# Fourteen tiles of x are turned by VectorE from square blocks instead of by TensorE, and the stage for v runs in the order in which it is written

## The chip, the cores and the metric

The kernel runs on one core of a Trainium2 chip. The metric is the device time of one execution in microseconds; three executions of the kernel before give a median of 1278.13 us (1277.75 to 1278.33).

The engines are called by the names of the profile: PE (matmuls on TensorE; PEld is its weight load), DVE (VectorE), ACT (ScalarE), POOL (GpSimd) and SP (SyncE, whose queue issues nearly all DMAs here). Each engine works through its own instructions in a fixed order.

## What is computed

One block of a network mixes two branches with a gate per token (B = 1, S = 2048 tokens, D = 512 channels, 32 heads of 16, F = 1792):

```python
x = A_x
g = _sigmoid((x * gate_w).sum(-1, keepdims=True))
a = _A_ref(x, A_wqkv, A_wo)                       # softmax attention, 32 heads of 16
b = _B_ref(x, B_w1, B_b1, B_w2, B_b2)             # layernorm, then an MLP across the tokens
return g * a + (1 - g) * b
```

What matters here is the beginning of it: `v = x @ wqkv[:, 1024:1536]`, and for each token the gate's sum `(x * gate_w).sum(-1)` and the mean and variance of its row. All matmul operands are float32 values split into a rounded part `hi` and a rest `lo`; a product is the sum of three matmuls, `hi*hi + hi*lo + lo*hi`.

## The kernel before

The 2048 tokens are 16 tiles of 128 rows. TensorE contracts over the partitions, so x is needed with its channels on the partitions: `xt_hi` and `xt_lo`, 128 partitions by 4 chunks of channels by 2048 tokens. They are kept, since the projections for k and q use them too.

The first stage makes them and v. For a tile t:

- `load(t)` brings the 128 rows of x, 2 KB each, as one DMA of 256 KB on SP's queue. Six buffers rotate; a buffer is free again when `row_stats` of its tile is done.
- `turn(t)` is four transposes of 128 by 128 on PE into one PSUM bank (line 201). `turned(t)` splits the bank: ACT copies it into `xt_hi` (line 82), DVE subtracts that from the bank into `xt_lo` (line 83).
- `products` adds up twelve matmuls of 512 columns (line 90) for v, three for each of the four chunks of channels. `v_out(t)` copies the bank into `v` on ACT (line 235).
- `row_stats(t)` on DVE reads the rows of x as they were loaded: BN_STATS (line 212), BN_AGGR (line 213) and a product with `gate_w` that also sums (line 215).

The weights for v come in four chunks of 128 channels, `wv_raw0` to `wv_raw3`, split by ACT and DVE into `wv_hi` and `wv_lo` (`split_wv`). Tiles 0 and 1 are done first and by hand: their matmuls (line 268, `part`) go chunk by chunk, in the order in which the weights arrive. This head is under `manual_schedule`, in which each engine's instructions stand in the order in which the program writes them. From tile 2 on the loop

```python
for t in range(2, NS):
    if t + 4 < NS: load(t + 4)
    if t + 1 < NS: turn(t + 1)
    if t == 4: biases(pool)
    if t in (8, 12): qk_w.append(wcols(qk_cols.pop(0)))
    row_stats(t - 2)
    ps = bank(); products(ps, v_pairs(t)); v_out(t, ps)
```

is left to a scheduler, which places each instruction when its operands can be there. It may pull a call forward out of its place in the text: POOL's fills of the two bias tiles (line 224), the two small loads of the biases (line 225) and the fill of `v` (line 296) are written late and stand early in their engines' order. In `biases` each of the two bias vectors is loaded into a cleared 128 by 128 tile, turned by a transpose on PE (line 227) and copied out by DVE (line 228).

`wcols` loads and splits the weights of one block of k or q, 128 columns as 512 pieces of 512 bytes (line 172). The stage after (line 90 again, `wc_hi` and `wc_lo`) projects k and q from `xt_hi` and `xt_lo`; then come the first layer of the MLP, attention with the rest of the MLP between its matmuls, and the output. None of that is touched.

Each DMA on SP's queue has one of eight semaphores in turn and waits for the DMA that had it before, so that at most eight are under way.

Of the kernel before, what the change touches and what calls it, by code (L numbers as in the profile page):

```python
# [10 lines left out]
F32 = mybir.dt.float32  # L11
# [4 lines left out]
ALU = mybir.AluOpType  # L16
# [6 lines left out]
P = 128  # L23
S = 2048
D = 512
F = 1792
H = 32
DH = 16
NS = S // P
ND = D // P  # L30
NF = F // P
NB = 512
NQ = S // NB
VC = DH + 1
SCALE = DH**-0.5
# [40 lines left out]
def gated_mix(ctx: ExitStack, tc: tile.TileContext, a_x, a_wqkv, a_wo, b_w1, b_b1, b_w2, b_b2, gate_w, out):  # L76
    nc = tc.nc
    xf, of = (t.rearrange("b s d -> (b s) d") for t in (a_x, out))

    def split(hi, lo, src, copy, sub):  # L80

        copy(hi, src)  # L82
        return sub(lo, src, hi.bitcast(F32), ALU.subtract)  # L83

    def products(ps, pairs, start=True, stop=True):

        n, last = 0, 3 * len(pairs) - 1
        for (lh, ll), (rh, rl) in pairs:
            for a, b in ((lh, rh), (lh, rl), (ll, rh)):
                nc.tensor.matmul(ps, a, b, start=start and n == 0, stop=stop and n == last)  # L90
                n += 1
# [7 lines left out]
    ident = const.tile([P, P], F32, name="ident")  # L99
# [3 lines left out]
    z = const.tile([P, NS], F32, name="z")  # L103
# [9 lines left out]
    v = v_pool.tile([P, NS, H, VC], F32, name="v")  # L113
# [21 lines left out]
    loaded, ready, subs = [], [], []  # L135
# [27 lines left out]

    qk = qk_ctx.enter_context(tc.tile_pool(name="qk", bufs=2, side="right"))

    def wcols(c0):
# [3 lines left out]
        src = a_wqkv[:, c0 : c0 + P].rearrange("(k p) c -> p k c", p=P)  # L170
        with tc.issue_after(x_load.ins):
            nc.sync.dma_start(raw, src)
        split(hi, lo, raw, nc.scalar.copy, nc.gpsimd.tensor_tensor)
        return hi, lo

    qk_cols = [c0 + b * P for b in range(ND) for c0 in (D, 0)]
    qk_w = []
    x_load = None

    with tc.tile_pool(name="vp", bufs=1, side="right") as pool:  # L180
        xs = {}

        def load(t):
            nonlocal x_load
            xs[t] = pool.tile([P, D], F32, name="x", bufs=6)
            x_load = nc.sync.dma_start(xs[t], xf[t * P : (t + 1) * P, :])  # L186

        gw = pool.tile([P, D], F32, name="gw")
        wv = []

        def load_wv(k):
            raw = pool.tile([P, D], F32, name=f"wv_raw{k}")
            nc.sync.dma_start(raw, a_wqkv[k * P : (k + 1) * P, 2 * D : 3 * D])  # L193
            wv.append((raw, pool.tile([P, D], F32R, name=f"wv_hi{k}"), pool.tile([P, D], F32R, name=f"wv_lo{k}")))

        turns = {}

        def turn(t, later=False):
            turns[t] = acc.tile([P, ND, P], F32, name="acc")
            for k in range(ND):  # L200
                nc.tensor.transpose(turns[t][:, k, :], xs[t][:, k * P : (k + 1) * P], ident)  # L201
            if not later:
                turned(t)

        def turned(t):
            cols = slice(t * P, (t + 1) * P)
            split(xt_hi[:, :, cols], xt_lo[:, :, cols], turns[t], nc.scalar.copy, nc.vector.tensor_tensor)

        def row_stats(t):

            st = pool.tile([P, 6], F32, name="stats", bufs=3)
            tc.keep_in_program_order(nc.vector.bn_stats(st, xs[t]))
            nc.vector.bn_aggr(mv[:, t, :], st)
            junk = pool.tile([P, D], F32, name="junk")
            dot = nc.vector.scalar_tensor_tensor(
                junk, xs[t], 1.0, gw, ALU.mult, ALU.mult, accum_out=z[:, t : t + 1]
            )
            tc.keep_in_program_order(dot)

        def biases(pool):  # L220
            for n, (src, dst, rows, mul) in enumerate(((b_b1, b1, NF, 1.0), (b_b2, b2x2, NS, 2.0))):

                t = pool.tile([P, P], F32, name=f"bias{n}")
                nc.gpsimd.memset(t, 0.0)
                nc.sync.dma_start(t[:rows], src.rearrange("(r c) -> r c", c=P))
                pt = bank()[:, :P]
                nc.tensor.transpose(pt, t, ident)
                nc.vector.tensor_scalar_mul(dst, pt[:, :rows], mul)

        def v_pairs(t):  # L230
            cols = slice(t * P, (t + 1) * P)
            return [((xt_hi[:, k, cols], xt_lo[:, k, cols]), wv[k][1:]) for k in range(ND)]

        def v_out(t, ps):
            nc.scalar.copy(v[:, t, :, 0:DH], ps.rearrange("p (h d) -> p h d", d=DH))

        with tc.manual_schedule():

            idle = pool.tile([P, NB], BF16, name="idle")
            nc.vector.memset(idle, 0.0)  # L240
            warm_ps = bank()

            def warm(n):
                for _ in range(n):
                    nc.tensor.matmul(warm_ps, idle[:, :P], idle, start=True, stop=True)

            warm(6)
            load(0)
            load_wv(0)
            load_wv(1)  # L250
            load(1)
            load_wv(2)
            load_wv(3)
            for t in (2, 3):
                load(t)
            nc.sync.dma_start(gw, gate_w[None, :].broadcast_to([P, D]))

            def split_wv(k):
                raw, hi, lo = wv[k]
                split(hi, lo, raw, nc.scalar.copy, nc.vector.tensor_tensor)  # L260


            two_ps = [bank(), bank()]

            def part(k, *which, last=False):

                for n, (t, a, b) in enumerate(which):
                    nc.tensor.matmul(  # L268
                        two_ps[t],
                        (xt_hi, xt_lo)[a][:, k, t * P : (t + 1) * P],  # L270
                        wv[k][1 + b],
                        start=k == 0 and a == b == 0,
                        stop=last and n >= len(which) - 2,
                    )
# [24 lines left out]
        for t in range(2, NS):  # L299
            if t + 4 < NS:  # L300
                load(t + 4)
            if t + 1 < NS:
                turn(t + 1)
            if t == 4:
                biases(pool)
            if t in (8, 12):
                qk_w.append(wcols(qk_cols.pop(0)))
            row_stats(t - 2)
            ps = bank()
            products(ps, v_pairs(t))  # L310
            v_out(t, ps)
        for t in range(NS - 2, NS):
            row_stats(t)
# [41 lines left out]
    with tc.tile_pool(name="ln0", bufs=3, side="right") as ln:  # L355
# [18 lines left out]
        for b in range(ND):  # L374
# [3 lines left out]
            for n in range(NQ):  # L378
                ps = project(wk_b, n)
# [4 lines left out]
            for n in range(NQ):  # L384
                ps = project(wq_b, n)
# [795 lines left out]
```

## Time and profile before

| what | value |
|---|---|
| median of three executions | 1278.13 us |
| the profiled execution, span from first to last instruction | 1276.0 us |
| PE busy | 1266.6 us, 99% |
| DVE, ACT, POOL busy | 719.3, 1071.9, 210.8 us |
| mean granted TensorE clock | 0.999 |
| line 201, transposes of x on PE | 64 instructions, 9.7 us of pipelined time |

The median lies 2.1 us above the span of the profiled execution: the span counts from the first instruction to the last, the device time holds the start and end around them. Matmuls overlap in the pipe, so a busy time of PE is longer than the time by which it advances; the chain of waits, where each piece ends when the next can go on, gives the pace. A row of the timeline gives the start, the duration, the engine, the line, the operation, what it writes and reads, how many rows were merged, and in brackets how long the engine sat idle and for whom.

### The profile page before, as it was taken

Reading aid. Unit: us, or ns where it says so; the run is one execution under the profiler, and the core shown is the slowest. Engines: PE = TensorE matmul, PEld = TensorE weight load, DVE = VectorE, ACT = ScalarE, POOL = GpSimd, SP = SyncE. Lnnn points to the kernel's source line nnn. Section 1 sums busy time; section 2 is a strip of 40 time slices with the busy share of each in tenths; the row PEclk is TensorE's granted clock in tenths of the full one; section 3 lists DMA queues with packets and bytes.
Section 4 is the critical chain, followed back from the end, with each engine's and each line's share of the span. In section 5 each row is a group of like instructions: output and inputs, shape, how many; then the busy total and the mean of one; then the engine's idle time right before and its main releaser. Section 6 shows DMA issues by size and latency. Waiting matters only on the chain.

```text
span 1276.0 us, 33051 instructions
## 1 busy us (share of the span) xinstructions
PE 1266.6 (99%) x13278; PEld 801.2 (63%) x13278; DVE 719.3 (56%) x1329; ACT 1071.9 (84%) x1484; POOL 210.8 (17%) x435
## 2 busy tenths in 40 slices
PE   9999999999999999999999999999999999999998
PEld 7888888886555555555555555555555555555555
DVE  5675363528776766666634346676666662325425
ACT  3444343437999999999999999999999999999994
POOL 0210144454111111111110011111111111100000
PEclk9999999999999999999999999999999999999999
DMA  4497743328443333433555533333343345446721
GB/s 133 141 304 274 241 122 99 99 71 166 84 93 59 74 76 70 79 70 76 116 107 115 129 77 69 69 72 76 68 78 72 74 82 109 98 88 198 149 62 70
DMA packets 94641, 137.37 MB, mean 108 GB/s; under 512 B 16313, under 2 KB 55375, under 8 KB 91408
## 3 DMA queue, kind: packets, MB, share of 16 engines
q1 hardware_dynamic: 93904, 134.14, 44.8%
q8 instruction: 106, 1.74, 0.6%
q10 hardware_dynamic: 576, 1.05, 0.2%
q14 instruction: 55, 0.45, 0.1%
HBM read 99.10 MB, written 36.03 MB: 106 GB/s over the span
## 4 chain that ended last, share of the span: by engine, by line
PE 99%; DMA 0%; ACT 0%; SPq 0%; DVE 0%; issue 0%
PE s L826 37%; PE s L868 34%; PE acc L429 12%; PE acc L90 10%; PE dn L989 4%; PE pa L1060 1%; PE acc L201 1%; PE dn L857 0%; PE acc L268 0%; DMA x<-in_A_x_dram 0%; ACT pt L891 0%; PE pa L1069 0%; SPq L193 0%; DVE base L1082 0%; SPq L186 0%
## 5 line engine op out<-in xcount | busy, mean ns | idle before, releaser
L891 ACT ACTIVATE pt<-s 128x512 f32<-128x512 f32 (+1 forms) x1259 | 943.5, 962 | 10.0 <-PE s L868 4.3
L868 PE MATMUL s<-qs,ks 64*128 64x512 f32 x2048 | 493.9, 404 | 0.8 <-POOL token L993 0.5
L826 PE MATMUL s<-pt,v 128*17 128x256 f32 x8024 | 482.6, 381 | 0.0
L868 PEld LDWEIGHTS s<-qs,ks 64*128 64x128 f32 x2048 | 325.4, 184 | 168.7 <-ACT pt L891 91.0
L846 DVE TENSOR_TENSOR ot<-s,ot 128x256 f32<-128x256 f32 (+2 forms) x427 | 190.4, 447 | 348.9 <-PE s L826 271.6
L826 PEld LDWEIGHTS s<-pt,v 128*17 128x17 f32 x8024 | 210.4, 97 | 232.2 <-ACT pt L891 84.2
L989 PE MATMUL dn<-u_hi,w_hi 64*128 64x512 f32 x428 | 186.4, 436 | 0.0
L83 POOL TENSOR_TENSOR w_lo<-w_raw,w_hi 128x512 fp32r<-128x512 f32 (+1 forms) x126 | 149.7, 1189 | 167.3 <-ACT w_hi L82 107.3
L989 PE MATMUL dn<-u_lo,w_hi 64*128 64x512 f32 x430 | 169.8, 395 | 0.0
L989 PE MATMUL dn<-u_hi,w_lo 64*128 64x512 f32 x430 | 169.2, 394 | 0.0
L993 POOL MEMSET token<- 1x1 f32 x256 | 26.2, 102 | 779.4 <-PE dn L989 711.8
L913 DVE SCALAR_TENSOR_TENSOR row<-row,o_hi 128x512 f32<-128x512 f32 x168 | 116.6, 694 | 4.9
L82 ACT CAST w_hi<-w_raw 128x512 fp32r<-128x512 f32 (+1 forms) x67 | 38.1, 569 | 79.4 <-PE acc L429 58.9
L429 PE MATMUL acc<-h_hi,w_hi 128*128 128x512 f32 x224 | 87.1, 389 | 0.0
L429 PE MATMUL acc<-h_lo,w_hi 128*128 128x512 f32 x224 | 87.1, 389 | 0.0
L429 PE MATMUL acc<-h_hi,w_lo 128*128 128x512 f32 x224 | 87.1, 389 | 0.0
L989 PEld LDWEIGHTS dn<-u_hi,w_lo 64*128 64x128 f32 x430 | 79.3, 184 | 1.3
L989 PEld LDWEIGHTS dn<-u_lo,w_hi 64*128 64x128 f32 x430 | 79.4, 185 | 0.4
L989 PEld LDWEIGHTS dn<-u_hi,w_hi 64*128 64x128 f32 x428 | 78.6, 184 | 1.1
L90 PE MATMUL acc<-xt_hi,wc_hi 128*128 128x512 f32 x128 | 49.8, 389 | 0.0
L90 PE MATMUL acc<-xt_lo,wc_hi 128*128 128x512 f32 x128 | 49.8, 389 | 0.0
L90 PE MATMUL acc<-xt_hi,wc_lo 128*128 128x512 f32 x128 | 49.8, 389 | 0.0
(145 smaller groups left out, 1148.5 us busy)
## 6 DMA issues: line engine op xcount, KB each, us to landing
w_raw<-in_B_w_dram SPq DMA_DIRECT2D x96, 256.0 KB
ks<-kp SPq DMA_DIRECT2D x192, 128.0 KB
qs<-qp SPq DMA_DIRECT2D x256, 64.0 KB
qp<-pc SPq DMA_DIRECT2D x16, 768.0 KB
x<-in_A_x_dram SPq DMA_DIRECT2D x32, 256.0 KB
kp<-pc SPq DMA_DIRECT2D x16, 512.0 KB
w_raw<-in_B_w_dram SPq DMA_DIRECT2D x32, 128.0 KB
bp<-row SPq DMA_DIRECT2D x16, 256.0 KB
```

The costliest lines, as they stand in the source:

```text
L82: copy(hi, src)
L83: return sub(lo, src, hi.bitcast(F32), ALU.subtract)
L90: nc.tensor.matmul(ps, a, b, start=start and n == 0, stop=stop and n == last)
L201: nc.tensor.transpose(turns[t][:, k, :], xs[t][:, k * P : (k + 1) * P], ident)
L429: nc.tensor.matmul(p, a, b, start=first and k == 0, stop=last and k == 2)
L826: mm = nc.tensor.matmul(av[32 * j : 32 * j + VC, i * QC : (i + 1) * QC], v[:, c, g % NP * 2 + i, :], pt[:, h * QC : (h + 1) * QC], start=t ...
L846: reads(nc.vector.tensor_tensor(x, y, x, ALU.add), bank)
L868: mm = nc.tensor.matmul(banks[:, bank, :], kt[grp][rows, c * P : (c + 1) * P], qt[grp][rows, qb * NB : (qb + 1) * NB], start=True, stop=True,)
L891: act = nc.scalar.activation(dst, banks[:, at[0] : at[-1] + 1, :], AF.Exp, scale=SCALE)
L913: nc.vector.scalar_tensor_tensor(box[1], q or box[1], a, x, ALU.add, ALU.mult)
L989: mm = nc.tensor.matmul(ps, a[half], b[half], start=first and not second, stop=last and bool(second))
L993: fence = nc.gpsimd.memset(token, 0.0)
```

## The change

Tiles 2 to 15 are no longer turned by PE. `load_blocks(t)` reads the tile of x once more, as four DMAs of 64 KB: the quarter q of the channels goes to partitions 32q to 32q + 31, each with four pieces of 128 columns (512 bytes), one for each group of 32 rows. `turn_blocks(t)` lets DVE transpose 32 by 32 blocks within each band of 32 partitions, 128 by 512 in one instruction, into `xw` in SBUF; ACT copies that into `xt_hi` and POOL (no longer DVE) subtracts for `xt_lo`. A partition now holds one channel out of every four neighbours per chunk: chunk k has the channels 4p + k. For that, the transposes of tiles 0 and 1 read every fourth column of x, DVE's transpose reads every fourth element of a piece, and the rows of the weights for v, k and q are loaded in the same dealing.

The rows of x are still loaded, later, for `row_stats` alone, with five buffers in place of six.

The whole loop moves into `manual_schedule`, with `turn_blocks(t + 2)` first, two tiles ahead; the k and q weights are loaded at t = 6 and 9 and split at t = 9 and 12. The warm-up matmuls go round three PSUM banks.

```diff
+        QUARTERS = P // BLOCK
+        blocks_of = {}
+        def load_blocks(t):
+            blocks_of[t] = pool.tile([P, QUARTERS, P], F32, name="xb", bufs=4)
+            src = xf[t * P : (t + 1) * P, :].rearrange("(a r) (q c) -> q r a c", r=BLOCK, q=QUARTERS)
+            for q in range(QUARTERS):
+                nc.sync.dma_start(blocks_of[t][q * BLOCK : (q + 1) * BLOCK], src[q])
+        def turn_blocks(t):
+            cols = slice(t * P, (t + 1) * P)
+            whole = pool.tile([P, ND, P], F32, name="xw", bufs=2)
+            nc.vector.transpose(
+                whole.rearrange("p k (a r) -> p k a r", r=BLOCK), blocks_of.pop(t).rearrange("p a (c k) -> p k a c", k=ND)
+            )
+            split(xt_hi[:, :, cols], xt_lo[:, :, cols], whole, nc.scalar.copy, nc.gpsimd.tensor_tensor)
...
             for t in (2, 3):
+                load_blocks(t)
+            nc.sync.dma_start(gw, gate_w[None, :].broadcast_to([P, D]))
+            for t in (4, 5):
+                load_blocks(t)
+            for t in (2, 3, 4):
                 load(t)
-            nc.sync.dma_start(gw, gate_w[None, :].broadcast_to([P, D]))
...
             split_wv(2)
             part(2, *both)
+            turn_blocks(2)
             split_wv(3)
-            turn(2)
             part(3, *both, last=True)
+            turn_blocks(3)
             for t in range(2):
                 v_out(t, two_ps[t])
-        nc.gpsimd.memset(v[:, :, :, DH:VC], 1.0)
-        load(4)
-        load(5)
-        for t in range(2, NS):
...
+            nc.gpsimd.memset(v[:, :, :, DH:VC], 1.0)
+            for t in range(2, NS):
+                if t + 2 < NS:
+                    turn_blocks(t + 2)
+                row_stats(t - 2)
+                if t + 4 < NS:
+                    load_blocks(t + 4)
+                if t + 3 < NS:
+                    load(t + 3)
+                if t == 4:
+                    biases(pool)
+                if t in (6, 9):
+                    qk_w.append(load_wcols(qk_cols.pop(0)))
+                if t in (9, 12):
+                    qk_w.append(split_wcols(*qk_w.pop(0)))
+                ps = bank()
+                products(ps, v_pairs(t))
+                v_out(t, ps)
+            for t in range(NS - 2, NS):
+                row_stats(t)
```

In the lists that follow a row is an instruction with its line, what it writes and reads, and in brackets the engines or DMA semaphores that it waits for; numbers behind names tell buffers apart, and a count at the end stands for like rows in succession.

POOL at the start of the program, before:

```order
L296 MEMSET v 128x512
masks.py:199 ISA
masks.py:199 AFFINE_SELECT ident<-ident 128x128 [waits Pool_49]
L224 MEMSET bias_272 128x128
L224 MEMSET bias_278 128x128
L83 TENSOR_TENSOR wc_lo<-wc_raw,wc_hi 128x512 [waits DMAHW4_49,Activation_49]
```

And with the change (the tiles of `xt_lo` here are 2 and 3, then 4, 5 and 6, then 7 to 11):

```order
masks.py:199 AFFINE_SELECT ident<-ident 128x128 [waits Pool_49]
L84 TENSOR_TENSOR xt_lo<-xw,xt_hi 128x4x128 [waits Activation_49] x2
L323 MEMSET v 128x512
L84 TENSOR_TENSOR xt_lo<-xw,xt_hi 128x4x128 [waits Activation_49] x3
L246 MEMSET bias_303 128x128
L246 MEMSET bias_309 128x128
L84 TENSOR_TENSOR xt_lo<-xw,xt_hi 128x4x128 [waits Activation_49] x5
```

The fills of the bias tiles stood behind the identity matrix and now stand behind the subtraction for tile 6.

ACT from the last split of the v weights on, before (`acc_186`, `acc_209`, `acc_237`, `acc_265` are the turned tiles 2 to 5; the copies into `v` are those of tiles 0 to 3):

```order
L82 CAST wv_hi2_131<-wv_raw2_129 128x512 [waits DMAHW4_49]
L82 CAST wv_hi3_135<-wv_raw3_133 128x512 [waits DMAHW5_49]
L82 CAST xt_hi_97<-acc_186 128x4x128 [waits PE_49]
L235 COPY v_87<-acc_142 128x32x16 [waits PE_49]
L235 COPY v_87<-acc_143 128x32x16 [waits PE_49]
L82 CAST xt_hi_97<-acc_209 128x4x128 [waits PE_49]
L235 COPY v_87<-acc_221 128x32x16 [waits PE_49]
L82 CAST xt_hi_97<-acc_237 128x4x128 [waits PE_49]
L235 COPY v_87<-acc_249 128x32x16 [waits PE_49]
L82 CAST xt_hi_97<-acc_265 128x4x128 [waits PE_49]
```

And with the change (`xw_208`, `xw_220`, `xw_227`, `xw_257`, `xw_287` are tiles 2 to 6; `acc_273` is the bank of tile 3):

```order
L83 CAST wv_hi2_133<-wv_raw2_131 128x512 [waits DMAHW4_49]
L83 CAST xt_hi_97<-xw_208 128x4x128 [waits DVE_49]
L83 CAST wv_hi3_137<-wv_raw3_135 128x512 [waits DMAHW5_49]
L83 CAST xt_hi_97<-xw_220 128x4x128 [waits DVE_49]
L257 COPY v_87<-acc_166 128x32x16 [waits PE_49]
L257 COPY v_87<-acc_167 128x32x16 [waits PE_49]
L83 CAST xt_hi_97<-xw_227 128x4x128 [waits DVE_49]
L257 COPY v_87<-acc_243 128x32x16 [waits PE_49]
L83 CAST xt_hi_97<-xw_257 128x4x128 [waits DVE_49]
L257 COPY v_87<-acc_273 128x32x16 [waits PE_49]
L83 CAST xt_hi_97<-xw_287 128x4x128 [waits DVE_49]
```

Tile 2's cast went ahead of the cast of the last v weights, and the cast of a tile t + 3 stands behind the copy out of tile t.

PE around the two bias transposes, before (`acc_249` is tile 3's bank, `acc_289` tile 4's):

```order
L90 MATMUL acc_249<-wv_hi3_135,xt_lo_98 128x512
L201 MATMUL acc_265<-ident_69,x_205 128x128 [waits DMAHW2_49,PE_49]
L201 MATMUL acc_265<-ident_69,x_205 128x128 x3
L227 MATMUL acc_275<-ident_69,bias0_272 128x128 [waits DMAHW3_49,PE_49,Pool_49]
L227 MATMUL acc_281<-ident_69,bias1_278 128x128 [waits DMAHW4_49,PE_49,Pool_49]
L90 MATMUL acc_289<-wv_hi0_121,xt_hi_97 128x512 [waits Activation_49]
```

And with the change (`acc_273` tile 3, `acc_315` tile 4):

```order
L91 MATMUL acc_273<-wv_lo3_138,xt_hi_97 128x512
L91 MATMUL acc_273<-wv_hi3_137,xt_lo_98 128x512
L249 MATMUL acc_306<-ident_69,bias0_303 128x128 [waits DMAHW1_49,PE_49,Pool_49]
L249 MATMUL acc_312<-ident_69,bias1_309 128x128 [waits DMAHW2_49,PE_49,Pool_49]
L91 MATMUL acc_315<-wv_hi0_123,xt_hi_97 128x512 [waits Activation_49]
```

The transposes of the tile are gone, and the bias transposes stand where they stood, between tiles 3 and 4.

More of the change, by code (lines that the diff above doesn't have):

```diff
@@ L32 @@
 NB = 512
+BLOCK = 32
 NQ = S // NB
@@ L164, in gated_mix, with load_wcols @@
     qk = qk_ctx.enter_context(tc.tile_pool(name="qk", bufs=2, side="right"))
-    def wcols(c0):
+    def load_wcols(c0):
         raw = qk.tile([P, ND, P], F32, name="wc_raw")
@@ L169, in wcols, with split_wcols @@
         lo = qk.tile([P, ND, P], F32R, name="wc_lo", bufs=3)
-        src = a_wqkv[:, c0 : c0 + P].rearrange("(k p) c -> p k c", p=P)
-        with tc.issue_after(x_load.ins):
-            nc.sync.dma_start(raw, src)
+        src = a_wqkv[:, c0 : c0 + P].rearrange("(p k) c -> p k c", k=ND)
+        nc.sync.dma_start(raw, src)
+        return raw, hi, lo
+    def split_wcols(raw, hi, lo):
         split(hi, lo, raw, nc.scalar.copy, nc.gpsimd.tensor_tensor)
         return hi, lo
+    def wcols(c0):
+        with tc.issue_after(x_load.ins):
+            loaded = load_wcols(c0)
+        return split_wcols(*loaded)
     qk_cols = [c0 + b * P for b in range(ND) for c0 in (D, 0)]
@@ L184, in load @@
             nonlocal x_load
-            xs[t] = pool.tile([P, D], F32, name="x", bufs=6)
+            xs[t] = pool.tile([P, D], F32, name="x", bufs=5)
             x_load = nc.sync.dma_start(xs[t], xf[t * P : (t + 1) * P, :])
@@ L192, in load_wv @@
             raw = pool.tile([P, D], F32, name=f"wv_raw{k}")
-            nc.sync.dma_start(raw, a_wqkv[k * P : (k + 1) * P, 2 * D : 3 * D])
+            nc.sync.dma_start(raw, a_wqkv.rearrange("(p k) c -> p k c", k=ND)[:, k, 2 * D : 3 * D])
             wv.append((raw, pool.tile([P, D], F32R, name=f"wv_hi{k}"), pool.tile([P, D], F32R, name=f"wv_lo{k}")))
@@ L200, in turn @@
             for k in range(ND):
-                nc.tensor.transpose(turns[t][:, k, :], xs[t][:, k * P : (k + 1) * P], ident)
+                nc.tensor.transpose(turns[t][:, k, :], xs[t].rearrange("p (r k) -> p k r", k=ND)[:, k, :], ident)
             if not later:
@@ L207, in turned @@
             split(xt_hi[:, :, cols], xt_lo[:, :, cols], turns[t], nc.scalar.copy, nc.vector.tensor_tensor)
+        QUARTERS = P // BLOCK
[12 more added lines that the diff above has]
+            split(xt_hi[:, :, cols], xt_lo[:, :, cols], whole, nc.scalar.copy, nc.gpsimd.tensor_tensor)
         def row_stats(t):
             st = pool.tile([P, 6], F32, name="stats", bufs=3)
-            tc.keep_in_program_order(nc.vector.bn_stats(st, xs[t]))
+            nc.vector.bn_stats(st, xs[t])
             nc.vector.bn_aggr(mv[:, t, :], st)
             junk = pool.tile([P, D], F32, name="junk")
[L215 to L218, printed above, removed]
+            nc.vector.scalar_tensor_tensor(junk, xs[t], 1.0, gw, ALU.mult, ALU.mult, accum_out=z[:, t : t + 1])
         def biases(pool):
@@ L240, in gated_mix @@
             nc.vector.memset(idle, 0.0)
-            warm_ps = bank()
+            warm_ps = [bank() for _ in range(3)]
             def warm(n):
-                for _ in range(n):
-                    nc.tensor.matmul(warm_ps, idle[:, :P], idle, start=True, stop=True)
+                for i in range(n):
+                    nc.tensor.matmul(warm_ps[i % 3], idle[:, :P], idle, start=True, stop=True)
             warm(6)
@@ L290, in gated_mix @@
             part(2, *both)
+            turn_blocks(2)
             split_wv(3)
-            turn(2)
             part(3, *both, last=True)
+            turn_blocks(3)
             for t in range(2):
                 v_out(t, two_ps[t])
-        nc.gpsimd.memset(v[:, :, :, DH:VC], 1.0)
-        load(4)
-        load(5)
-        for t in range(2, NS):
[L300 to L313, printed above, removed]
+            nc.gpsimd.memset(v[:, :, :, DH:VC], 1.0)
[18 more added lines that the diff above has]
+                row_stats(t)
         pool.tile([P, 40], F32, name="pad")
```

## The prediction

> **What bounds the kernel now.** I read the page first (share of each engine), then the chain of waits in order of time over the first 120 us, then the timeline of single engines there.
>
> ```profile
> span 1276.0 us, 33051 instructions
> PE 1266.6 (99%) x13278; PEld 801.2 (63%) x13278; DVE 719.3 (56%) x1329; ACT 1071.9 (84%) x1484; POOL 210.8 (17%) x435
> ```
>
> PE is busy for 99% of the span, so time is won or lost where PE's work or its waits change. The chain shows the stage for v (start, length, whose work):
>
> ```profile
> 11.40 0.44 PE acc L201 x4
> 11.83 1.39 PE acc L268 x6
> 13.22 0.44 PE acc L201 x4
> 13.66 2.77 PE acc L90 x12
> 16.43 0.44 PE acc L201 x4
> 16.87 2.77 PE acc L90 x12
> 19.64 0.44 PE acc L201 x4
> 20.07 0.22 PE acc L227 x2
> 20.29 2.74 PE acc L90 x12
> ...
> 51.89 0.44 PE acc L201 x4
> 52.33 67.82 PE acc L90 x299
> ```
>
> Nothing but PE stands in it: a tile is 2.77 us of matmuls for v and 0.44 us of transposes, 3.21 us, and the next stage follows without a gap. From 52.33 us PE runs through two more v tiles and the k and q projections. The rest of the program has the same order on PE, so whatever the stage gains or loses arrives at the end in full.
>
> **Part by part.** *Removed from PE*: the transposes of fourteen tiles, 14 x 0.44 = 6.16 us. That is the whole possible gain.
>
> *The head.* These rows hold ACT and DVE before tile 2:
>
> ```profile
> 8.22 1.15 ACT L82 CAST wv_hi<-wv_raw 128x512 fp32r<-128x512 f32 x2
> 8.96 1.28 DVE L83 TENSOR_TENSOR wv_lo<-wv_raw,wv_hi 128x512 fp32r<-128x512 f32 x2
> 11.59 0.70 PE L268 MATMUL acc<-wv_hi,xt_hi 128*128 128x512 f32 x2
> ```
>
> Now tile 2's cast, which waits for DVE's transpose, comes before the cast of the last v weights. DVE ends the third weights' rest at about 9.6 us (half of the second row); with a transpose of 1.0 us (below) that gives 10.65, tile 2's cast 0.58 later (half of the first row) 11.25, the weights' cast 11.85. The six matmuls of the last `part` then start 0.3 us later than now (last row). They are followed by tile 2 with no transposes between: it starts 0.13 us earlier, where two removed turns (0.88) had promised more. The head gives back 0.75 us. If the transpose takes 0.7 us it gives back 0.4.
>
> *DVE's transpose.* The trace has one of half the size, dense, and one instruction on 512 elements that reads every fourth float:
>
> ```profile
> 1257.67 0.45 DVE L1029 STREAM_TRANSPOSE turned<-ot 128x256 f32<-128x256 f32 x1
> 179.81 1.04 DVE L413 TENSOR_REDUCE far<-most_row 1x32 f32<-1x512 f32 x1
> 180.89 1.19 DVE L414 TENSOR_SCALAR far<-far 1x32 f32<-1x32 f32 x1
> 66.05 0.68 DVE L372 TENSOR_REDUCE kmax<-acc 128x1 f32<-128x512 f32 x1
> ```
>
> Doubling the elements bounds it from below at about 0.7 and from above at 0.9 (twice the whole row); the stride may add the 0.36 us by which the second row exceeds the last. The third row makes me careful: 32 elements took 1.19 us there, so that place is slow for another reason too. I take 1.0, with 0.7 and 1.3 as ends. [...] The same stride is read by PE's eight transposes of tiles 0 and 1; nothing here prices it, between 0 and doubling the second turn (0.44); I take 0.
>
> *DVE, ACT and POOL per tile.*
>
> ```profile
> L212 DVE BATCH_NORM_STATS2 stats<-x 128x6 f32<-128x512 f32 x16 | 11.0, 685 | 0.0
> L215 DVE SCALAR_TENSOR_TENSOR junk<-x,gw 128x512 f32<-128x512 f32 x16 | 11.1, 693 | 0.0
> 16.47 0.59 ACT L235 COPY v<-acc 128x512 f32<-128x512 f32 x1 [1.88 <-PE acc L90]
> 16.95 0.59 ACT L82 CAST xt_hi<-acc 128x512 fp32r<-128x512 f32 x1
> 40.29 1.30 POOL L83 TENSOR_TENSOR wc_lo<-wc_raw,wc_hi 128x512 fp32r<-128x512 f32 x1 [37.87 <-ACT wc_hi L82]
> 58.37 0.68 DVE L212 BATCH_NORM_STATS2 stats<-x 128x6 f32<-128x512 f32 x1
> 59.77 0.69 DVE L212 BATCH_NORM_STATS2 stats<-x 128x6 f32<-128x512 f32 x1
> ```
>
> DVE: 1.40 us for a tile's statistics (the last two rows' distance) and 1.0 for the transpose, 2.4. ACT: two copies, 1.1. POOL: 1.3. All are under the 2.77 us that PE needs, and the transposes run two tiles ahead, so PE hides them: cost nothing. Without that cover, a DVE tile of 2.4 to 2.7 us would be the stage's pace anyway, still below 2.77.
>
> *The loads.* A tile now takes five DMAs:
>
> ```profile
> 1.21 0.89 SPq L193 DMA_DIRECT2D wv_raw<-in_A_wqkv_dram  x2
> 36.34 0.43 SPq L172 DMA_DIRECT2D wc_raw<-in_A_wqkv_dram  x1
> 16.70:19.30 2.60, 2.60 (x14) 2.13 (x13) 1.70 (x6) 0.84 (x2) 0.00 (x0) 1.00 0.33 101
> 36.30:39.30 3.00, 3.00 (x17) 2.43 (x16) 2.06 (x5) 0.87 (x3) 0.00 (x0) 1.00 0.66 175
> ```
>
> SP needs 0.45 us for each (first row), 2.25 us a tile. The last two rows end in DMA share and GB/s: one load of x filled 2.60 x 0.33 = 0.86 us of the sixteen DMA engines, a load of x with one of the same size in 512-byte pieces 3.00 x 0.66 = 1.98. That pair is what a tile needs, 1.98 of 2.77 us. Both fit, SP closely. They are hidden as long as SP isn't held up.
>
> *The biases.* Here is the price of the program order. Before, POOL cleared the tiles and SP loaded them long before PE asked:
>
> ```profile
> 2.08 0.35 POOL L224 MEMSET bias<- 128x128 f32 x2
> 7.08 0.98 SPq L225 DMA_DIRECT2D bias<-in_B_b_dram  x2
> ```
>
> Now the fills stand on POOL behind tile 6's subtraction, which waits for tile 6's cast on ACT, which stands behind the copy out of tile 3; that waits for tile 3's last matmul, and PE's next instructions are the bias transposes. So PE waits for a chain that starts when PE itself stops. From the rows above: copy 0.5, cast 0.6, hand-over 0.1, subtraction 1.3, both fills 0.35, that is 2.85 us. Then the loads. A small load with a waiting reader is here:
>
> ```profile
> 1233.85 0.32 SPq L796 DMA_DIRECT2D rc<-s  x1
> 1236.10 0.19 DVE L799 TENSOR_SCALAR rc<-rc 96x64 f32<-96x64 f32 x1 [1.44 <-DMA rc<-s]
> ```
>
> From issue to use 2.25 us; the second load is issued 0.49 us after the first (half of 0.98), which starts when the first fill ends: 2.7 + 0.49 + 2.25, and the transpose: 5.5 us of wait. Ends: 5.0 if a 7 KB load lands 0.5 sooner than that one of 24 KB; 7 if it queues behind the load of x and the blocks issued just ahead (0.86 us of DMA). I take 6.2. Behind these instructions wait, on SP, the blocks of tile 9, on DVE the transpose of tile 7, on ACT the copy out of tile 4. Tiles 4, 5 and 6 are split by then, so PE can go on with them while the others catch up.
>
> *PE after the wait.* No row of before has PE idle for more than 1.2 us, so the trace can't say how it resumes. It shows how PE starts from rest:
>
> ```profile
> L245 PE MATMUL acc<-idle x8: 379/634/634, 1.2 to 4.4; 128*128 128x512 bf16 x8
> 1.21 2.74 PE L245 MATMUL acc<-idle 128*128 128x512 bf16 x6 [1.21 <-DVE idle L240]
> ```
>
> Six matmuls took 2.74 us where twelve take 2.77 later, 634 ns each and 379 at the end: half pace for about 3 us (the granted clock reads 1.00 there all the same). If PE falls back to it in the wait, three to five microseconds at half pace lose 1.4 to 2.5 us; I take 2.0, against 0 if it doesn't. [...]
>
> **The sum.** -6.16 + 0.75 + 6.2 + 2.0 = +2.8 us. The profiled execution's 1276.0 would become 1278.8; with the 2.1 us around it, 1281.0 us against the median of 1278.13.
>
> **The rivals.**
>
> *The wait alone.* The bias wait is there, but PE resumes at full pace: +0.8, or down to -0.3 with a fast transpose and a wait of 5.5: 1278.5 us. For it: no row says that 6 us of rest suffice. Against it: PE at the program's start, also after a rest, begins at half pace.
>
> *SP becomes the bound.* If a block load with its four pieces per partition takes SP 0.55 us or more, five of them are 2.75 us and SP sets the pace, the bias loads come later and every tile waits: at 0.6 us, 3.0 - 2.77 = 0.23 for ten tiles, 2.3 us, and about 1 us more before the biases (four issues and two, each 0.15 longer), 2.8 + 2.3 + 1 = +6.1: 1284 us. Against it: 512 pieces took SP 0.43 us, not more than 128.
>
> *Faster.* The biases don't hold PE: then 6.16 less 0.4 remains, 1272.4 us. The result is beyond 0.2% faster only if the wait is below 3.2 us (6.16 - 0.4 - 2.56). The engines' part alone is 2.85, so the loads would have to land in 0.35 us; the row has 2.25. This decides against it unless POOL's fills run earlier than their place.
>
> **How the numbers follow.** Forecast 47%, wait alone 28%, SP 16%, faster 9%. A measurement of this kernel tells about 0.2%, 2.56 us, from no change: the bounds are 1275.6 and 1280.7. The forecast has its own range of 1279.4 to 1283, of which about seven tenths lie above 1280.7 (34%); with SP's 16% and a tail of the second case (2%), slower is 52%. Same is 13 + 26 + 1 = 40%, faster 8%. The range goes from 1277.4 (wait alone, short) to 1283.8.
>
> **What would show it.** Right: in the waits of PE one entry of 5 to 7 us at line 249, for a DMA or POOL, after tile 3; tiles 2.77 us apart elsewhere; the first matmuls after it 634 ns long. DVE's transpose at line 229 tells 0.7 from 1.0. Wrong: no such entry (then faster); several shorter waits at line 91 for POOL or ACT (then SP, DVE or the loads are the bound, and SP's rows at line 224 are longer than 0.55); full pace directly after the wait (then about 1278.5).

## The result and the profile after

The changed kernel takes 1281.93 us (median of seven runs, 1280.38 to 1283.0); the kernel before, run beside it, 1277.88 us (1277.53 to 1278.76). The ratio is 1.0031 with a 95% interval of 1.0020 to 1.0041: slower by 0.3%, some 4 us. The profiled execution took 1281.8 us, with a span of 1280.0 us against 1276.0 before.

The page of the changed kernel, first the shares of the engines:

```profile
span 1280.0 us, 33041 instructions
PE 1263.3 (99%) x13222; PEld 796.5 (62%) x13222; DVE 727.3 (57%) x1329; ACT 1072.1 (84%) x1484; POOL 229.2 (18%) x449
```

PE has 56 instructions and 3.3 us of busy time less than before, and the span is 4.0 us longer: the transposes went, and something else came. The list of PE's waits in the first 70 us (engine, line, whom it waited for, total, times, longest) says what:

```profile
PE acc L249 <- DMA bias<-in_B_b_dram: 6.7, 1, 6.7
...
PE acc L294 <- ACT wv_hi L83: 1.0, 1, 1.0
PE acc L294 <- DVE wv_lo L84: 0.2, 1, 0.2
```

Left out is the start of the program, which was there before. New are 6.7 us at the bias transposes and 1.2 us in the head, at the last v weights. PE's timeline shows these places, the first matmul of tile 2, the end of tile 3 and the first projection of k and q, which marks the end of the stage:

```profile
12.35 0.72 PE L294 MATMUL acc<-wv_hi,xt_hi 128*128 128x512 f32 x2 [1.04 <-ACT wv_hi L83]
...
14.30 0.39 PE L91 MATMUL acc<-wv_hi,xt_hi 128*128 128x512 f32 x1
...
19.52 0.39 PE L91 MATMUL acc<-wv_hi,xt_lo 128*128 128x512 f32 x1
26.57 0.75 PE L249 MATMUL acc<-ident,bias 128*128 128x128 f32 x2 [6.67 <-DMA bias<-in_B_b_dram]
26.97 0.77 PE L91 MATMUL acc<-wv_hi,xt_hi 128*128 128x512 f32 x1
...
30.53 0.43 PE L91 MATMUL acc<-wv_hi,xt_lo 128*128 128x512 f32 x1
...
61.40 0.39 PE L91 MATMUL acc<-xt_hi,wc_hi 128*128 128x512 f32 x1
```

The same two landmarks before:

```profile
13.41 0.48 PE L90 MATMUL acc<-wv_hi,xt_hi 128*128 128x512 f32 x1
...
57.65 0.39 PE L90 MATMUL acc<-xt_hi,wc_hi 128*128 128x512 f32 x1
```

Tile 2 starts 0.89 us later and the stage ends 3.75 us later, nearly all of the 4.0 by which the span grew. After the wait the matmuls are about 630 ns long until 30.5 us, and 390 again from then on. The windows of 1 us around that show the granted clock, the third number from the end:

```profile
27.00:28.00 1.00, 1.00 (x5) 0.81 (x5) 0.79 (x3) 0.00 (x0) 0.00 (x0) 0.50 0.62 110
...
31.00:32.00 1.00, 1.00 (x6) 0.82 (x5) 0.97 (x4) 0.33 (x1) 0.00 (x0) 1.00 0.87 233
```

So the balance of the stage, from rows of both traces:

| term | predicted | measured | from |
|---|---|---|---|
| fourteen turns gone | -6.16 | -6.76 | 0.88 in the head, then 12 x 0.49: a tile starts 2.72 us after the last, 3.21 before |
| the head gives back | +0.75 | +1.77 | tile 2 0.89 later, where 0.88 earlier was possible |
| wait for the biases | +6.2 | +7.0 | 19.75, where tile 4 could have started at the pace of tiles 2 and 3 (14.30 and two tiles of 2.72), to its first matmul (26.97), less 0.22 for the transposes |
| half pace | +2.0 | +1.79 | twelve matmuls 26.97 to 31.48 = 4.51, less 2.72 |
| sum | +2.8 | +3.8 | |

### The profile page after: what moved, and what is told of

It reads as the page before. It is cut to its first block, busy times and chain, and to the rows that moved or that the text cites. A ratio compares the mean times of both kernels' runs of the same rounds, so it can differ in the third digit from the quotient of the medians.

```text
span 1280.0 us, 33041 instructions
## 1 busy us (share of the span) xinstructions
PE 1263.3 (99%) x13222; PEld 796.5 (62%) x13222; DVE 727.3 (57%) x1329; ACT 1072.1 (84%) x1484; POOL 229.2 (18%) x449
## 3 DMA queue, kind: packets, MB, share of 16 engines
q8 instruction: 106, 1.74, 0.6%
q10 hardware_dynamic: 576, 1.05, 0.2%
## 4 chain that ended last, share of the span: by engine, by line
PE 96%; DMA 2%; SPq 0%; ACT 0%; DVE 0%; POOL 0%; issue 0%; DVEq 0%
PE s L855 37%; PE s L897 34%; PE acc L458 12%; PE acc L91 9%; PE dn L1018 3%; PE pa L1089 1%; DMA wv_raw<-in_A_wqkv_dram 0%; DMA w_raw<-in_B_w_dram 0%; DMA xb<-in_A_x_dram 0%; DMA gw<-in_gate_w_dram 0%; ACT pt L920 0%; PE pa L1098 0%; SPq L194 0%; DMA qs<-qp 0%; SPq L224 0%; POOL xt_lo L84 0%
```

## The experiments

The question was whether the wait at the biases, with the slow clock behind it, is all that made the loss; what sets its length; and where the head's time went. Each kernel below is compared with the kernel before on the same chip (1277.7 to 1277.9 us there).

**The bias loads alone, moved forward** (the changed kernel otherwise).

```diff
+        bias_tiles = []
+        def load_biases(pool):      # fill and load of both tiles
...
+        def biases(pool):           # transposes and copies out, as before
...
             for t in (2, 3, 4):
                 load(t)
+            load_biases(pool)
```

> The two bias tiles are cleared and loaded at the end of the first loads, ahead of the loop; everything else is the change as it is. Theory (the biases hold PE, and the rest of the wait is the slow pace after it): no wait at the bias transposes, no matmul of 634 ns after the start, and the 7.0 us between tiles 3 and 4 and the 1.7 us of half pace are gone: 1281.9 - 8.7 = 1273.2 us, clearly faster than before. Rival (the stage is also bound by its loads or by DVE, and the wait for the biases only hides it): PE waits for POOL or ACT at tiles 6 to 9, 2 to 5 us in all, and the time is 1275 to 1279 us.

1274.04 us (1273.4 to 1274.7), ratio 0.9968 (0.9955 to 0.9980), span 1272.2: faster than the kernel before by 0.3%, a little short of the 1273.2 us expected. PE's waits are those of the head and nothing at the biases. The wait and its half pace are worth 7.9 us, the difference of the two medians; the sum over the stage gave 8.8. Part of the difference is lost behind the stage. The first layer of the MLP starts at 139.99 us here, against 144.85 in the kernel before and 148.60 in the changed one: 4.9 us ahead of the kernel before, of which 3.8 are left at the end of the span. Of the 1.1 us lost on the way, 0.5 is a wait of PE for DVE at line 893 (292.8 us), which neither of the other two has; where the rest goes was not traced.

**The wait kept, but PE kept busy** with 26 matmuls on zeros between tile 3 and the biases.

```diff
                 if t == 4:
+                    fill_ps = bank()
+                    for _ in range(26):
+                        nc.tensor.matmul(fill_ps, idle[:, :P], idle, start=True, stop=True)
                     biases(pool)
```

> The change, with 26 matmuls on zeros (their result is used by nothing) on PE between tile 3 and the bias transposes, about 5.9 us at full pace inside a wait of 6.7 us. Theory (PE falls to half pace because it rested): the bias transposes start where they did, near 26.6 us, the granted clock stays at 1.0, the matmuls of tile 4 take 390 ns, and the time is 1.7 to 2.0 us less, 1280.0 us. Rival (the slow matmuls come from something else at that place, loads or DVE and POOL at work): the eight matmuls stay at 634 ns and the time at 1281.9 us.

1280.16 us (1279.04 to 1281.24), ratio 1.0018 (1.0009 to 1.0028). PE's timeline and a window behind the wait:

```profile
19.67 5.79 PE L335 MATMUL acc<-idle 128*128 128x512 bf16 x26
25.90 0.53 PE L249 MATMUL acc<-ident,bias 128*128 128x128 f32 x2 [0.44 <-DMA bias<-in_B_b_dram]
...
27.00:28.00 1.00, 1.00 (x6) 0.78 (x5) 1.00 (x2) 0.00 (x0) 0.00 (x0) 1.00 0.33 95
```

The biases come at 25.9 us, still some 6 us after tile 3 ends, but the granted clock stays at 1.00 and every matmul behind takes 390 to 400 ns. 1.8 us come back, about what the half pace had cost in the changed kernel (1.79). The biases are also 0.67 us earlier in this profile, though nothing on SP or POOL was changed; the blocks of tile 6 landed earlier too, as shown below. Work that computes nothing made the kernel faster, by those 1.8 us.

**The head alone**: the last v weights are split ahead of the transpose of tile 2.

```diff
-            turn_blocks(2)
             split_wv(3)
+            turn_blocks(2)
             part(3, *both, last=True)
```

> The change, with the split of the last v weights ahead of the turning of tile 2, so that the cast of the weights no longer waits for DVE's transpose. Tile 2's matmuls then start about 1.5 us earlier (14.3 becomes 12.8). Theory of the prediction (the wait for the biases starts when PE stops after tile 3): everything moves with it, 1280.4 us. Rival (the biases come from a chain of loads and DVE that PE doesn't set: the blocks of tile 6 land at 20.8 us, then transpose, cast, subtraction, fills, loads): the bias transposes stay at 26.6 us, the wait grows by 1.5 us, and the time stays at 1281.9 us.

1282.24 us (1279.57 to 1282.71), ratio 1.0029 (1.0018 to 1.0041): no better. PE's timeline, first and last matmul of the disturbed stretch and the biases between:

```profile
12.83 0.39 PE L91 MATMUL acc<-wv_hi,xt_hi 128*128 128x512 f32 x1
...
25.78 0.66 PE L249 MATMUL acc<-ident,bias 128*128 128x128 f32 x2 [6.92 <-DMA bias<-in_B_b_dram]
...
30.93 0.52 PE L91 MATMUL acc<-wv_hi,xt_lo 128*128 128x512 f32 x1
```

Tile 2 starts 1.47 us earlier, so the order of these two calls held most of the head's loss. PE loses 0.4 us of that again at the third matmul of tile 2, the first to read `xt_lo`, so its stop behind tile 3 comes 1.05 us earlier (18.70). The biases come 0.8 us earlier, and half pace lasts longer: twelve slow matmuls where there were nine. These times alone do not tell what the chain to the biases starts from, since in the kernel with 26 matmuls on zeros the biases came 0.67 us earlier with PE's stop where it was. The rival's forecast, biases still at 26.6 us and a wait longer by 1.5, is not met either (25.78, and 0.25 longer). What sets the time shows in the chain of waits of the changed kernel (start, length, whose work):

```profile
16.61 4.21 DMA xb<-in_A_x_dram
...
20.94 1.09 DVE xw L229
...
22.06 0.63 ACT xt_hi L83
...
22.76 1.76 POOL xt_lo L84
24.51 0.17 POOL bias L246 x2
24.68 1.75 DMA bias<-in_B_b_dram
...
26.57 0.75 PE acc L249 x2
```

and in ACT's rows, the copy out of tile 3 and the cast of tile 6:

```profile
19.94 0.58 ACT L257 COPY v<-acc 128x512 f32<-128x512 f32 x1 [1.00 <-PE acc L91]
22.06 0.62 ACT L83 CAST xt_hi<-xw 128x512 fp32r<-128x512 f32 x1 [1.53 <-DVE xw L229]
```

The blocks of tile 6 go out by 16.6 us and land at 20.8; their transpose, cast and subtraction stand ahead of the fills on POOL. The copy out of tile 3 is long over when the cast of tile 6 starts: ACT then waited 1.53 us for DVE, and DVE for the blocks. The two profiles with the biases earlier fit this: the blocks of tile 6 land at 19.67 us with the head's edit and at 19.91 with the 26 matmuls on zeros, and the bias transposes follow 6.1 and 6.0 us later, 5.75 in the changed kernel. From PE's stop the three distances are 7.1, 6.2 and 6.8. SP's queue hangs on the same blocks: the rows of tile 7, which stand ahead of the bias loads, are issued at 23.43 us, when DVE is through with the statistics of tile 2, and these stand on DVE behind the transpose of tile 6. So of the wait for POOL's fills (first bias load issued at 24.68) only 0.9 us is POOL's own.

**Both edits.**

> Both edits: biases loaded early and the last v weights split before tile 2 is turned. Theory (two separate losses of PE): 1.5 us less than with early biases alone, 1271.7 us. Rival (PE then runs into the loads of tiles 6 and 7): waits of 1 to 2 us at line 91 for POOL, and the same time as with early biases alone.

1273.68 us (1273.22 to 1274.04), ratio 0.9966 (0.9953 to 0.9978); the span is 1272.2, the same as with the early biases alone. Tile 2 starts at 12.56, and PE then waits 0.97 us for the biases:

```profile
19.60 0.57 PE L255 MATMUL acc<-ident,bias 128*128 128x128 f32 x2 [0.97 <-DMA bias<-in_B_b_dram]
```

SP's rows and the chain show why:

```profile
13.85 1.38 SPq L194 DMA_DIRECT2D x<-in_A_x_dram  x3
15.34 0.82 SPq L248 DMA_DIRECT2D bias<-in_B_b_dram  x2
```

```profile
15.34 4.12 DMA bias<-in_B_b_dram
```

The two small loads land 4.1 us after the first of them is issued, behind three loads of 256 KB. The head's gain was all but handed back: tile 2 starts 1.9 us earlier than with the early biases alone, tile 4 only 0.1 (19.93 and 20.04). The rest went into this wait and into a stop of PE for POOL's subtraction of tile 2. After this wait of 1 us there is no half pace: the matmuls behind it take 390 to 480 ns.

**The kernel before, with its loop put in program order** (PE's transposes kept; the weights for k and q are loaded and split at the same t as in the change; the diff is shortened).

```diff
-        for t in range(2, NS):
-            if t + 4 < NS: load(t + 4)
-            if t + 1 < NS: turn(t + 1)
+            for t in range(2, NS):          # inside manual_schedule
+                if t + 1 < NS: turn(t + 1)
+                row_stats(t - 2)
+                if t + 4 < NS: load(t + 4)
                 if t == 4: biases(pool)
...
-            row_stats(t - 2)
```

> The kernel before, PE's transposes kept, with only its loop put in program order. Theory (the loss lies in the order alone, not in the turns on DVE): the two bias loads now stand on SP behind the load of tile 8, which waits for the statistics of tile 2, and these stand on DVE behind the subtraction of tile 5, whose transposes are PE's last work before the biases. Cast 0.6, subtraction 0.7, statistics 1.4, issues 0.9, landing 1.75 to 2.25: PE waits 5 to 6 us at the biases and goes on at half pace for 1.5 to 2 us, 1284.5 to 1286 us. Rival (the order is harmless by itself, only the block loads and POOL's subtraction make the wait): 1277 to 1279 us with no wait of PE over 1 us at the biases.

1286.63 us (1286.03 to 1287.13), ratio 1.0068 (1.0053 to 1.0083). Its PE at the biases, and its chain of waits ahead of them:

```profile
25.53 0.66 PE L233 MATMUL acc<-ident,bias 128*128 128x128 f32 x2 [5.82 <-DMA bias<-in_B_b_dram]
```

```profile
19.90 0.50 ACT xt_hi L82
...
20.42 0.69 DVE xt_lo L83
21.11 0.61 DVE stats L219
...
22.59 0.33 SPq L193
...
22.96 2.43 DMA bias<-in_B_b_dram
...
26.19 5.12 PE acc L90 x12
```

POOL has filled these bias tiles by 2.4 us, and still PE waits 5.8 us, then runs twelve matmuls in 5.12 us instead of 2.77. Here it is SP that stands still, since `load(8)` needs a buffer that `row_stats(2)` gives free. The order alone cost 8.8 us (1286.63 less 1277.84), without a block load or a transpose on DVE; the forecast of 1284.5 to 1286 fell a little short. In the change, too, it is the order that loses, through the biases' place: with that place mended it gains 3.9 us (1277.9 less 1274.04).

**The changed kernel with its loop left to the scheduler.**

```diff
-            for t in range(2, NS):
+        for t in range(2, NS):      # outside manual_schedule
```

> The change with its loop left to the scheduler as it was before. The fills of the bias tiles are back at the start on POOL, the bias loads still stand on SP behind the rows of tile 7, which wait for the statistics of tile 2 on DVE. Theory (two queues hold the biases, POOL's and SP's, so freeing one changes little): the loads go out about 1 us earlier, PE still waits 5 to 6 us at the biases with half pace behind it, 1280 to 1281.5 us. Rival (the fills' place on POOL alone makes the wait): no wait over 1 us there, 1274 us.

1281.28 us (1278.28 to 1282.88), ratio 1.0026 (1.0017 to 1.0036). The fills are back at 0.9 and 1.4 us, so POOL's place holds nothing up. The rows on SP and on PE:

```profile
22.92 0.38 SPq L194 DMA_DIRECT2D x<-in_A_x_dram  x1
23.40 0.82 SPq L247 DMA_DIRECT2D bias<-in_B_b_dram  x2
```

```profile
26.61 0.66 PE L249 MATMUL acc<-ident,bias 128*128 128x128 f32 x2 [4.02 <-DMA bias<-in_B_b_dram]
```

The loads go out directly behind the rows of tile 7, 1.3 us earlier than in the changed kernel (24.68), land 3 us later instead of 1.75, and PE resumes at 26.6 us as it did there. Its wait is 4.0 us, less than the 5 to 6 forecast, because PE comes to the biases 2.7 us later: in the head it waited 2.4 us where a statistics instruction of DVE, itself waiting for the rows of tile 1, was put ahead of the rest of the v weights. Two queues held the biases, and freeing one of them moved nothing.

**The stride in DVE's transpose**, measured by itself: the transpose reads each piece as it lies.

```diff
-    blocks_of.pop(t).rearrange("p a (c k) -> p k a c", k=ND)
+    blocks_of.pop(t).rearrange("p a (k c) -> p k a c", k=ND)
```

> The change with DVE's transpose reading each piece of a block as it lies, 128 neighbouring floats, instead of every fourth; the channels are then dealt otherwise than in the weights, so the output is not the product wanted. If the stride costs, the transpose takes 0.7 to 0.9 us instead of 1.10; if the instruction costs 1.1 us at this size whatever it reads, it stays at 1.1. The time should stay within 1280 to 1282.5 either way, since the transpose is a small part of the chain to the biases (at most 0.4 us less).

A single execution took 1281.5 us. The transposes of both kernels (count; shortest, median, longest in ns), the changed one first:

```profile
L229 DVE STREAM_TRANSPOSE xw<-xb x14: 1055/1100/1117, 10.0 to 51.3; 128x512 f32<-128x512 f32 x14
```

```profile
L229 DVE STREAM_TRANSPOSE xw<-xb x14: 699/709/714, 10.0 to 51.0; 128x512 f32<-128x512 f32 x14
```

Reading every fourth float costs 0.39 us per transpose here, 1.10 for 0.71. PE's wait at the biases hardly changes, 6.8 us for 6.7.

**The biases still earlier**, ahead of the load of `gate_w`, with both edits:

```diff
+            load_biases(pool)
             nc.sync.dma_start(gw, gate_w[None, :].broadcast_to([P, D]))
             for t in (4, 5):
                 load_blocks(t)
             for t in (2, 3, 4):
                 load(t)
-            load_biases(pool)
```

> As with both edits (early biases, and the last v weights split ahead of tile 2's transpose), but the two bias loads go out before the load of gate_w and the blocks of tiles 4 and 5, instead of behind the rows of tiles 2 to 4. Theory (the 0.97 us wait left at the biases was the queue of loads ahead of them, 4.1 us from issue to landing): no wait over 0.3 us there, 1272.6 to 1273.0 us. Rival (the head is bound by the tiles' chain, which returns any gain; or the blocks of tile 4 now come 0.9 us later and PE waits for them): 1273.5 to 1274 us, with a wait at line 91 for DVE, ACT or POOL in tiles 2 to 5.

1273.73 us (1273.41 to 1274.95), ratio 0.9970 (0.9958 to 0.9981): nothing gained, as the rival said. PE waits 0.39 us at the third matmul of tile 2 and has gaps of 0.1 to 0.3 us at the third matmul of tiles 6, 11 and 12, each time for POOL. The end of its chain:

```profile
17.77 3.82 DMA xb<-in_A_x_dram
...
21.72 1.10 DVE xw L229
...
22.84 0.63 ACT xt_hi L83
...
23.54 1.80 POOL xt_lo L84
...
25.38 34.73 PE acc L91 x150
```

The stage ends within 0.1 us of the same time in this kernel, with both edits and with the early biases alone (its last matmul for v starts at 52.70 to 52.79 us), though tile 4 started 1 us earlier here. So in these traces blocks, transpose, cast and subtraction arrive about as fast as PE needs them, and PE starting earlier only waits.

**POOL's subtraction** took 1.74 to 1.80 us for tiles 4 to 13 here, and 1.27 for tiles 2 and 3 (2.54 for both). The last kernel changes what DVE does when it starts:

```diff
             st = pool.tile([P, 6], F32, name="stats", bufs=3)
+            junk = pool.tile([P, D], F32, name="junk")
+            nc.vector.scalar_tensor_tensor(junk, xs[t], 1.0, gw, ALU.mult, ALU.mult, accum_out=z[:, t : t + 1])
             nc.vector.bn_stats(st, xs[t])
             nc.vector.bn_aggr(mv[:, t, :], st)
-            junk = pool.tile([P, D], F32, name="junk")
-            nc.vector.scalar_tensor_tensor(junk, xs[t], 1.0, gw, ALU.mult, ALU.mult, accum_out=z[:, t : t + 1])
```

> As the last kernel with the biases ahead of gate_w, but in row_stats DVE's product with gate_w (two operands in SBUF) comes directly behind the transpose, ahead of the two instructions of the batch norm, instead of behind them. In the trace of that kernel each subtraction of POOL starts 0.03 us after such a product and takes 1.78 to 1.80 us, against 1.29 where DVE runs something with one operand. Theory (the two engines don't read two SBUF operands at the same time: POOL stands still until DVE's product ends): the product is over when POOL starts, the subtractions take 1.25 to 1.33 us, the small stops of PE for xt_lo in tiles 6 to 12 (0.3 at 25.38 us, 0.2 twice) go, 1272.5 to 1273.2 us. Rival (POOL's subtraction takes 1.8 us beside any work of DVE): the subtractions stay at 1.7 to 1.8 us, 1273.5 to 1274 us.

1273.47 us (1272.49 to 1275.06), ratio 0.9963 (0.9950 to 0.9977). POOL's subtraction for tile 6 in the last kernel, then in this one:

```profile
23.54 1.79 POOL L84 TENSOR_TENSOR xt_lo<-xw,xt_hi 128x512 fp32r<-128x512 f32 x1 [2.19 <-ACT xt_hi L83]
```

```profile
23.79 1.29 POOL L84 TENSOR_TENSOR xt_lo<-xw,xt_hi 128x512 fp32r<-128x512 f32 x1 [1.64 <-ACT xt_hi L83]
```

The forecast of the subtractions is right and that of the time is not: they fall to 1.28 to 1.30 us, but for two (1.71 and 1.73), and the median moves by 0.3 us, less than the runs of one kernel scatter. PE's gap in tile 6 is gone, and in tile 12, where POOL also splits weights for k and q, and in tile 14 gaps of 0.1 to 0.3 us remain. But in the profiled execution of this kernel the rows of tile 1 came late, and PE reached tile 2 1.9 us later than in the last kernel. So this profile tells the length of the subtractions, not the total nor whether PE's gap went because of them. It shows one thing more, the wait for those rows and a window behind it:

```profile
7.79 0.85 PE L209 MATMUL acc<-ident,x 128*128 128x128 f32 x4 [1.08 <-DMA x<-in_A_x_dram]
...
9.00:10.00 1.00, 1.00 (x4) 0.79 (x3) 0.70 (x2) 0.78 (x2) 0.00 (x0) 0.50 0.42 82
```

Here the granted clock fell to 0.50 after a wait of only 1.1 us, though PE had been idle for parts of the 2 us before as well.

## Why the prediction was right

It forecast 1281.0 us against 1278.13, a loss of 2.9; the loss is 4.05. Point by point:

*The turns.* 0.44 us each were right as work, but not, as the prediction said, the whole possible gain: a tile without a turn is 0.49 shorter. The 0.05 more lies in the twelve matmuls themselves: 2.77 us in the chain before, 2.72 now, where they start 0.227 us apart.

*The head* was the worst-sized term, 0.75 for 1.77. The cast of tile 2 does stand ahead of the cast of the last v weights on ACT, as the prediction said; the last `part` started at 12.35 where it had 11.9, because DVE first waited 0.48 us for the blocks. Its six matmuls then took 1.95 us where the prediction had 1.39: DVE's rest of the last v weights took 1.35 us, twice the 0.68 of the third weights' rest, beside POOL's subtraction of tile 2 (see the last section). The edit of the head moved tile 2 forward by 1.47 us; so the order of these two calls is shown to be the cause, the split between its parts is read from one trace.

*The biases.* The place, the waiting queue and the size were right (6.2 for 7.0), and removing this wait gave 7.9 us back. The step that failed is the one that began it, "a chain that starts when PE itself stops". The chain begins with the blocks of tile 6, issued by 16.6 us and landed at 20.8, 1.1 us after PE stopped. ACT's rows show it: the cast of tile 6 waited for DVE's transpose and not for the copy out of tile 3. That 6.2 comes near 7.0 is partly luck, since two errors cancel, the start and the loads: the predicted chain had 2.85 us of engines and, to make up its 6.2, 3.35 for loads and transposes; from 20.9 us on the trace has 3.7 for the engines, POOL's subtraction with 1.76 instead of 1.3, and 2.0 for the loads. That the loads alone could decide, without POOL, the prediction did not price: on SP they also stand behind rows of x that wait for DVE's statistics, and the two kernels with early fills show 4.0 and 5.8 us of wait without POOL.

*Half pace.* 2.0 for 1.79, and the kernel that filled the wait gave 1.8 back. That a wait brings half pace was the author's estimate from the start of the program; no row of before showed it. The granted clock fell while PE stood still: it reads 0.88 from 23 to 24 us, with PE idle since 19.9, and 0.50 from there to 30, beside matmuls of 630 ns; at the start of the program it read 1.00 beside matmuls of 634 ns. Behind the waits of 4.0, 5.8, 6.7 and 6.9 us at the biases the runs show half pace, and behind the one of 0.97 us none. Two shorter ones in a head had it too: behind 2.4 us in the kernel left to the scheduler the matmuls at 11.07, 11.50 and 11.93 us take 630 ns, and behind the 1.1 us of the last kernel the clock reads 0.50. So no run here gives the idle time that is safe. The slow stretch at the biases lasted about seven matmuls to twelve and cost 1.4 to 2.5 us.

*DVE, SP and the loads in the steady part.* DVE's transpose is 1.10 us, between the two ends and near the 1.0 taken. PE's transposes with the stride do take longer in one place: the four of tile 0 advance PE by 0.89 us where they took 0.49 before (4.63 less 3.74, 4.23 less 3.74), those of tile 1 by 0.39 for 0.42 (0.51 in the kernel with the head's edit). It is not seen later, since `part` for the third weights starts no later than before (10.70 us for 10.78, its last pair), so the 0 taken was right for the time. SP is not the bound: after the wait PE never stops for it. In the kernels without that wait, though, "PE hides them: cost nothing" no longer holds exactly: the chain of blocks, DVE, ACT and POOL returns any gain of the head.

*The rivals.* The wait alone, without half pace, fell with the clock's 0.50; SP as the bound fell with tiles 2.72 us apart. The faster case needed the biases not to hold PE, and that is what the first experiment made: 1274.04 us, against 1272.4 in the prediction. Two things fall short of its 5.76 us. The stage gained 4.9, since the head gave back more and the turns gained more than was reckoned; and only 3.8 to 3.9 of that are left at the end. That "whatever the stage gains or loses arrives at the end in full" was nearly so for the loss (3.75 in the stage, 4.0 in the span) and not for the gain.

## What to carry to other kernels

When a loop goes from a scheduler into program order, look first at the small work that the scheduler had pulled out of it, here two loads of 7 and 8 KB that PE needs once: follow each through every queue it now stands in, since freeing one queue alone gave nothing and moving the calls to the start of the program gave 7.9 us. The waits of 4.0 to 6.9 us on PE cost their length and 1.4 to 2.5 us of half clock behind it, so if such a wait can't be removed it is worth filling (1.8 us here). And once PE's work has been thinned out, a microsecond won at the head is kept only if the chain that feeds PE can run faster too: here the 1.9 us by which tile 2 started earlier moved the end of the stage by less than 0.1.

## What the runs showed of the hardware

Where an instruction of DVE and one of POOL that each read two operands from SBUF overlapped here, one of them took longer: DVE's 1.35 us for 0.68, POOL's 1.76 to 1.80 for 1.29. In the changed kernel (POOL, then DVE):

```profile
11.86 1.27 POOL L84 TENSOR_TENSOR xt_lo<-xw,xt_hi 128x512 fp32r<-128x512 f32 x1 [10.53 <-ACT xt_hi L83]
```

```profile
8.88 0.68 DVE L84 TENSOR_TENSOR wv_lo<-wv_raw,wv_hi 128x512 fp32r<-128x512 f32 x1
...
12.33 1.35 DVE L84 TENSOR_TENSOR wv_lo<-wv_raw,wv_hi 128x512 fp32r<-128x512 f32 x1 [1.20 <-ACT wv_hi L83]
```

DVE starts at 12.33 while POOL runs, and ends 0.55 us after POOL's end at 13.13; with POOL idle it took 0.68 (at 8.88). The other way round POOL took 1.76 to 1.80 us when it started just behind the start of DVE's product with `gate_w`, and 1.29 (tile 6 in the last kernel) with that product moved out of the way, beside BN_STATS and DVE's transpose, which read one operand. What makes the later one wait is not shown.

The two bias loads, 7 and 8 KB, had landed 1.75 us after the first was issued in the changed kernel, 2.4 us after it in the kernel before in program order, 3.1 us after it in the kernel left to the scheduler, and 4.1 us after it behind three loads of 256 KB that were issued just ahead. An estimate from these four times is that a small load on SP's queue pays for what was issued shortly before it, here up to 2.4 us (4.1 less 1.75); no run changed that alone.
